# Column tiles of 64 for TensorE in a sliding-window attention with a dense block behind it

## The chip, the cores and the metric

The kernel runs on one core of a Trainium2 chip. The core has TensorE (matmuls, from SBUF into PSUM), VectorE, ScalarE, GpSimd and SyncE, which work from queues of their own and wait for one another through semaphores. The metric is the device time of one launch in microseconds (us), as the median of several runs. One further look is taken by the hardware profiler: its span runs from the first to the last instruction of one execution.

In the profile TensorE has two rows: PE for the matmul itself, which streams the moving operand through the array, and PEld for the load of the stationary operand ("weights") before it. A form such as "128\*128 128x512" gives the rows and columns of the stationary operand, and then partitions and columns of what is written.

## The reference

```python
# q, k, v: (8 batches, 8 heads, 576 positions, 64)
scores = q @ k.T / sqrt(64)
scores = where(abs(pos_q - pos_k) <= 32, scores, -1e9)
attn = exp(scores - max(scores)); attn /= sum(attn) + 1e-9
x = (attn @ v), heads side by side          # (8 * 576 = 4608 tokens, 512)
h = x @ w_in                                # (4608, 2048)
out = (relu(h) ** 2) @ w_out                # (4608, 512), float32
```

All arrays are given and returned in float32; the kernel's operands of TensorE are bfloat16, its sums in PSUM float32.

## The kernel before

**Attention.** Each batch is cut into 9 chunks of 64 queries, 72 steps n in all. The window of a chunk is 128 keys wide. `scores` (L471) computes the scores transposed, keys on partitions: for each of four pairs of heads j one matmul with the keys of the pair as stationary operand (128 keys in its columns) and the queries of both heads as 128 moving columns, where zeros in the unused rows of QZ keep the heads apart. ScalarE takes the exponential of all 512 columns (L484), and VectorE multiplies by the mask of the window into P (L491). P has for each pair of heads three blocks of 64 columns: head a, a block of zeros, head b.

`av` (L494) computes P V. For each pair of heads two matmuls add up in PSUM (L506, L507): columns [a, 0] of P as stationary operand against the values of head a, then [0, b] against those of head b. So rows 0 to 63 of the result are the 64 queries of head a and rows 64 to 127 those of head b. The moving operand has 64 value columns and one of ones, whose result is the sum for the softmax; VectorE takes its reciprocal (L522) and multiplies (L524) into XR. The zero blocks are written once, by `setup_ptz` (L305).

`xturn` (L529) turns XR so that features lie on partitions: for the first 28 steps by two transposes of TensorE into TRP (L542) and a copy by ScalarE, later by a DMA that SyncE issues.

**Q and K.** For the first two batches, `fine_turn` (L333) turns Q and K by TensorE: groups of 16 transposes with 48 stationary rows and 48 moving columns (L344). For the other batches VectorE transposes them in blocks (L434), and DMAs of SyncE spread them (L446, L454).

**Dense block.** A tile T is 512 tokens. For the first two tiles `mm1_small` (L551) works on 128 tokens at a time: 16 matmuls with 128 moving columns (L561). For the others `mm1` (L577) makes four matmuls with 512 moving columns for each of 16 slices of the hidden width (L584). ScalarE applies Relu, VectorE squares. `mm2` (L596) multiplies by w_out: 16 matmuls with 512 moving columns for each 128 tokens (L602), in four groups. ScalarE copies the result, SyncE stores it.

**Order.** Every operation is recorded with its engine, what it reads and writes, a due time (`key`) and an assumed duration (`dur`). `Prog.schedule` (L76) runs a list schedule over these and fixes the order on each engine; `emit` (L189) writes the instructions in that order with the waits that are needed. Attention is due 12 steps ahead of the dense block. In gaps that the plan leaves on TensorE early on, filler matmuls on zeros are placed (`idle`, L277); they write a PSUM buffer that nobody reads before it is overwritten. All durations are the planner's own numbers, 240 for the P V of a step, 230 for its scores, 864 for four matmuls of 512 columns.

A transfer is named by the queue that issues it: POOL for loads from memory, SP for the rest.

Of the kernel before, what the change touches and what calls it, by code (L numbers as in the profile page):

```python
# [7 lines left out]
BF16 = mybir.dt.bfloat16  # L8
# [9 lines left out]
VE = D_ + 1  # L18
# [6 lines left out]
TOFF, TST, TREL = 6, 0.9, 9  # L25
NQ = 48
PC = 4 * NQ


class Op:  # L30
# [198 lines left out]
class Gen:  # L229
# [5 lines left out]
    def alloc(self):  # L235
        nc = self.nc
        sb, ps = nc.alloc_sbuf_tensor, nc.alloc_psum_tensor
        self.SC = [ps(f"sc{i}", [128, 512], F32) for i in range(2)]
        self.AVP = ps("avp", [128, 512], F32)
        self.TRP = ps("trp", [128, 1024], BF16)  # L240
        self.HT = [ps(f"ht{i}", [128, 512], F32) for i in range(2)]
        self.OUTP = [ps(f"outp{i}", [128, 512], F32) for i in range(2)]

        self.RAW = {t: [sb(f"{t}raw{i}", [128, 9, 4, 64], BF16) for i in range(2)] for t in "qk"}
        self.ST = {t: sb(f"{t}st", [128, 2, 1152], BF16) for t in "qk"}
        self.QZ = [sb(f"qz{i}", [128, 4, 2, S_], BF16) for i in range(2)]
        self.KT = [sb(f"kt{i}", [128, 4, KW], BF16) for i in range(2)]
        self.VD = [sb(f"vd{i}", [128, 4, H_, VS], BF16) for i in range(2)]
        self.VX = [sb(f"vx{i}", [128, 5, H_, VS], BF16) for i in range(2)]
        self.MASK = [sb(f"mask{i}", [128, 64], BF16) for i in range(3)]  # L250
        self.ID = sb("ident", [128, 128], BF16)
        self.E = [sb(f"e{i}", [128, 512], BF16) for i in range(2)]
        self.PT = [sb(f"pt{i}", [128, 4 * 192], BF16) for i in range(2)]
        self.RS = [sb(f"rs{i}", [128, 4], F32) for i in range(2)]
        self.XR = [sb(f"xr{i}", [128, 256], BF16) for i in range(4)]
        self.XT = sb("xt", [128, NSTEP, 4, 64], BF16)
        self.W1 = sb("w1", [128, 4, DFF], BF16)
        self.W2 = sb("w2", [128, 16, DM], BF16)
        self.GT = [sb(f"gt{i}", [128, 16, 512], BF16) for i in range(2)]
        self.RT = [sb(f"rt{i}", [128, 512], BF16) for i in range(4)]  # L260
        self.ZZ = sb("zz", [128, 512], BF16)
        self.OE = [sb(f"oe{i}", [128, 512], F32) for i in range(3)]
# [10 lines left out]
    def setup_idle(self):  # L273

        self.ms("DVE", ["zz"], self.ZZ[:], 0.0, -1000, 200)
        self.p.idle_on = self.p.ops[-1]
        self.p.idle = lambda e: e.matmul(self.OUTP[1][:], self.ZZ[:, 0:128], self.ZZ[:], start=True, stop=True)  # L277

    def setup_id(self, key):
        self.ms("DVE", ["id"], self.ID[:], 1.0, key)  # L280
# [13 lines left out]
    def setup_rest(self, i, key):  # L294
# [6 lines left out]
        self.ms("DVE", [("vdone", i)], self.VD[i][:, :, :, 64:VS], 1.0, key, 120)  # L301
        self.ms("DVE", [("ktpad", i, 0)], self.KT[i][:, :, 0:32], 0.0, key)
        self.ms("DVE", [("ktpad", i, 1)], self.KT[i][:, :, 32 + S_:KW], 0.0, key)

    def setup_ptz(self, i, key):  # L305
        for j in range(4):
            self.ms("DVE", [("ptz", i)], self.PT[i][:, 192 * j + 64:192 * j + 128], 0.0, key, 70)

    def setup_qz(self, i, key, rows, old=()):

# [160 lines left out]
    def scores(self, n):  # L471
        b, c = divmod(n, NCH)
        i = b % 2
        sc = self.SC[n % 2]
        key = n - LEAD

        def f(e):
            for j in range(4):
                mm = e.matmul(sc[:, 128 * j:128 * j + 128], self.KT[i][:, j, 64 * c:64 * c + 128],  # L479
                              self.QZ[i][:, j, :, 64 * c:64 * c + 64], start=True, stop=True)  # L480
            return mm

        self.p.rec("PE", f, reads=self.qk_tags(b, c), writes=[("sc", n % 2)], key=key, dur=230)
        self.p.rec("ACT", lambda e: e.activation(self.E[n % 2][:], sc[:], ACTF.Exp, scale=0.125),  # L484
                   reads=[("sc", n % 2)], writes=[("e", n % 2)], key=key, dur=560)
        mi = 1 if c == 0 else (2 if c == NCH - 1 else 0)
        msk = self.MASK[mi]
        pt = bass.AP(self.PT[n % 2], 0, [[768, 128], [192, 4], [128, 2], [1, 64]])
        ee = bass.AP(self.E[n % 2], 0, [[512, 128], [128, 4], [64, 2], [1, 64]])
        mb = bass.AP(msk, 0, [[64, 128], [0, 4], [0, 2], [1, 64]])  # L490
        self.p.rec("DVE", lambda e: e.tensor_tensor(pt, ee, mb, ALU.mult),  # L491
                   reads=[("e", n % 2), ("mask", mi)], writes=[("pt", n % 2)], key=key, dur=430)

    def av(self, n):  # L494
        b, c = divmod(n, NCH)
        i = b % 2
        s = c // 2
        key = n - LEAD
        vt = self.VX[i][:, s] if c % 2 == 0 else self.VD[i][:, s]
        pt = self.PT[n % 2]  # L500

        def f(e):
            for j in range(4):
                ha = 4 * (j // 2) + j % 2
                o = self.AVP[:, VE * j:VE * j + VE]
                e.matmul(o, pt[:, 192 * j:192 * j + 128], vt[:, ha, 0:VE], start=True, stop=False)  # L506
                mm = e.matmul(o, pt[:, 192 * j + 64:192 * j + 192], vt[:, ha + 2, 0:VE], start=False, stop=True)  # L507
            return mm

        if c % 2 == 0:  # L510
            rd = [("vdone", i)]
            if s in (0, 4):
                rd += [("vx", i, s)]
            if s > 0:
                rd += [("vxl", i, s)]
            if s < 4 and not (b < 2 and s == 0):
                rd += [("vxh", i, s)]
        else:
            rd = [("vd", i, s), ("vdone", i)]
        self.p.rec("PE", f, reads=rd + [("pt", n % 2), ("ptz", n % 2)], writes=["avp"], key=key, dur=240)  # L520
        rs, xr = self.RS[n % 2], self.XR[n % 4]
        self.p.rec("DVE", lambda e: e.reciprocal(rs[:], bass.AP(self.AVP, 64, [[512, 128], [VE, 4]])),  # L522
                   reads=["avp"], writes=[("rs", n % 2)], key=key - 0.1, dur=160)
        self.p.rec("DVE", lambda e: e.tensor_tensor(  # L524
            bass.AP(xr, 0, [[256, 128], [64, 4], [1, 64]]), bass.AP(self.AVP, 0, [[512, 128], [VE, 4], [1, 64]]),
            bass.AP(rs, 0, [[4, 128], [1, 4], [0, 64]]), ALU.mult),
            reads=["avp", ("rs", n % 2)], writes=[("xr", n % 4)], key=key - 0.1, dur=430)

    def xturn(self, n):  # L529

        xr = self.XR[n % 4]
        key = n - LEAD
        old = [("fraw", 1, t, x) for t in "qk" for x in (1, 2)] if n >= 40 else []
        if n >= NPE:
            self.p.rec("SP", lambda e: e.dma_start(
                self.XT[:, n].rearrange("p (j h) q -> p j (h q)", j=2), xr[:], transpose=True),
                reads=[("xr", n % 4)], writes=[("xt", n)], dma=(f"x{n % 4}", n), key=key, dur=1000, move=(16, 20), old=old)
            return

        def f(e):  # L540
            for t in range(2):
                mm = e.transpose(self.TRP[:, 128 * t:128 * t + 128], xr[:, 128 * t:128 * t + 128], self.ID[:])  # L542
            return mm

        self.p.rec("PE", f, reads=[("xr", n % 4), "id"], writes=["trp"], key=key, dur=112)
        self.p.rec("ACT", lambda e: e.activation(self.XT[:, n], self.TRP[:, 0:256].rearrange("p (f q) -> p f q", f=4),
                                                 ACTF.Copy),
                   reads=["trp"], writes=[("xt", n)], key=key, dur=370)


    def mm1_small(self, T, g, q, key):  # L551
# [3 lines left out]
        ht, rt, gt = self.HT[k % 2], self.RT[k % 4], self.GT[T % 2]  # L555
        t0 = 512 * T + 128 * g

        def f(e):
            for d in range(4 * q, 4 * q + 4):
                for ft in range(4):  # L560
                    mm = e.matmul(ht[:, 128 * (d % 4):128 * (d % 4) + 128], self.W1[:, ft, 128 * d:128 * d + 128],  # L561
                                  self.XT[:, t0 // 64:t0 // 64 + 2, ft, :], start=(ft == 0), stop=(ft == 3))
            return mm

        self.p.rec("PE", f, reads=[("xt", 8 * T + 2 * g), ("xt", 8 * T + 2 * g + 1), ("w1", q)], writes=[("ht", k % 2)], key=key,
# [11 lines left out]
    def mm1(self, T, d, key):  # L577
# [3 lines left out]

        def f(e):
            for ft in range(4):
                mm = e.matmul(ht[:], self.W1[:, ft, 128 * d:128 * d + 128], self.XT[:, 8 * T:8 * T + 8, ft, :],  # L584
                              start=(ft == 0), stop=(ft == 3))
            return mm

        self.p.rec("PE", f, reads=[("xt", 8 * T + j) for j in range(8)] + [("w1", d // 4)], writes=[("ht", k % 2)],
# [7 lines left out]
    def mm2(self, T, u, seg, key):  # L596
# [2 lines left out]

        def f(e):  # L600
            for d in range(4 * seg, 4 * seg + 4):
                mm = e.matmul(op[:], gt[:, d, 128 * u:128 * u + 128], self.W2[:, d, :], start=(d == 0), stop=(d == 15))  # L602
            return mm

        self.p.rec("PE", f, reads=[("gt", T % 2, d, u) for d in range(4 * seg, 4 * seg + 4)] + [("w2", seg)],
# [10 lines left out]
    def build(self):  # L616
        p = self.p
# [6 lines left out]
        self.fine_load(0, "q", 0, K + 1)  # L624
        self.setup_id(K + 0.5)
        self.setup_rest(0, K + 1)
        self.setup_ptz(0, K + 1)
        self.setup_ptz(1, K + 1)
        self.load_ve(0, K + 2, False)
        self.setup_mask(1, K + 2.5)  # L630
        self.load_w1(0, K + 4)
# [115 lines left out]
```

## Time and profile before

| | before |
|---|---|
| median of three runs | 335.07 us |
| the three runs | 334.23, 335.07, 339.73 us |
| span of the profiled execution | 329.7 us |
| what lies around the span (median less span) | 5.4 us |
| TensorE busy, matmul | 312.8 us, 2707 instructions |
| TensorE busy, weight load | 176.9 us, 2707 instructions |
| VectorE busy | 201.8 us |
| ScalarE busy | 172.8 us |
| GpSimd busy | 82.5 us |
| mean granted clock of TensorE | 0.995 of full |

The profiled execution's whole time is not listed beside its span, so the fourth row is a difference against the median. Busy times overlap, and matmuls overlap one another: their ends are modelled, with a tail behind the stream. The rate of TensorE is therefore read from the starts of its instructions. The chain of work that ended last goes back from the last instruction, at each step to what released it, and says which work set the end. The waits say who waited for whom.

### The profile page before, as it was taken

The page shows a single profiled execution, that of the slowest core. Times are in us where ns is not written, and L with a number is a line of the kernel's source. Part 1 is how long each engine was busy: PE and PEld are TensorE (multiplying, and loading weights), DVE is VectorE, ACT ScalarE, POOL GpSimd, SP SyncE. Part 2 cuts the span into 40 slices and gives each one's busy share as a digit, 9 for nine tenths or more (in the row PEclk, how much of TensorE's full clock was granted, in tenths as well). Part 3 has the DMA queues.
Part 4 walks back from the last instruction along what each step waited for, and adds up shares of the span by engine and source line. Part 5 has one row for each costly group of instructions (what it writes and reads, how often), then busy time and mean ns, then how long its engine had stood idle before and what let it go on. Part 6 is the DMA issues. An engine that isn't in the chain of part 4 may idle for free.

```text
span 329.7 us, 6908 instructions
## 1 busy us (share of the span) xinstructions
PE 312.8 (95%) x2707; PEld 176.9 (54%) x2707; DVE 201.8 (61%) x461; ACT 172.8 (52%) x313; POOL 82.5 (25%) x130
## 2 busy tenths in 40 slices
PE   7699897999799999989899999999999999999996
PEld 3356496786685555445455555555555554444442
DVE  7546564989689788779777767777544442222200
ACT  2366279965574764555264555554455554434411
POOL 8999253125053242405321110000000000000000
PEclk9989999999999999999999999999999999999999
DMA  8999999999999999799999668333311111100012
GB/s 92 173 202 203 193 150 184 182 237 199 213 184 164 210 144 126 94 224 172 173 196 150 125 123 148 89 85 84 86 49 48 51 55 55 43 32 34 32 72 88
DMA packets 89376, 42.53 MB, mean 129 GB/s; under 512 B 54528, under 2 KB 83840, under 8 KB 89344
## 3 DMA queue, kind: packets, MB, share of 16 engines
q0 software_dynamic: 62272, 18.49, 61.1%
q1 hardware_dynamic: 27072, 23.60, 28.2%
q8 instruction: 21, 0.34, 0.5%
q14 instruction: 11, 0.09, 0.1%
HBM read 36.96 MB, written 9.44 MB: 141 GB/s over the span
## 4 chain that ended last, share of the span: by engine, by line
PE 81%; DMA 7%; DVE 6%; ACT 2%; issue 1%; POOL 1%; SPq 1%; ACTq 0%
PE outp L602 34%; PE ht L584 28%; PE ht L561 7%; PE sc L479 5%; DMA qz<-qst 4%; DMA qraw<-in_k_dram 2%; PE avp L507 2%; PE avp L506 2%; DVE qz L266 2%; PE outp L277 1%; DMA xt<-xr 1%; PE sc L344 1%; PE trp L542 1%; DVE qst L434 1%; SPq L454 1%
## 5 line engine op out<-in xcount | busy, mean ns | idle before, releaser
L602 PE MATMUL outp<-w,gt 128*128 128x512 bf16 x576 | 143.1, 379 | 0.9 <-DVE gt L570 0.9
L584 PE MATMUL ht<-xt,w 128*128 128x512 bf16 x448 | 113.5, 379 | 0.9 <-DMA xt<-xr 0.9
L590 ACT ACTIVATE rt<-ht 128x512 bf16<-128x512 f32 x112 | 66.9, 597 | 80.9 <-PE ht L584 77.7
L602 PEld LDWEIGHTS outp<-w,gt 128*128 128x128 bf16 x576 | 53.7, 98 | 59.1 <-DVE gt L570 1.5
L592 DVE TENSOR_TENSOR gt<-rt 128x512 bf16<-128x512 bf16 x112 | 46.3, 420 | 50.0 <-ACT rt L590 49.4
L584 PEld LDWEIGHTS ht<-xt,w 128*128 128x128 bf16 x448 | 40.7, 98 | 40.1 <-DMA xt<-xr 1.4
L484 ACT ACTIVATE e<-sc 128x512 bf16<-128x512 f32 x72 | 41.6, 596 | 18.5 <-PE sc L479 12.4
L381 POOL DMA_DIRECT2D vd<-in_v_dram x32 | 28.8, 911 | 84.0 <-PE avp L507 63.3
L491 DVE TENSOR_TENSOR pt<-e,mask 128x512 bf16<-128x512 bf16 x72 | 29.9, 416 | 16.5 <-ACT e L484 15.9
L434 DVE STREAM_TRANSPOSE kst<-kraw 128x640 bf16<-128x640 bf16 (+1 forms) x24 | 35.0, 1457 | 0.6 <-DMA kt<-kst 0.6
L434 DVE STREAM_TRANSPOSE qst<-qraw 128x640 bf16<-128x640 bf16 (+1 forms) x24 | 35.1, 1462 | 0.0
L611 ACT ACTIVATE oe<-outp 128x512 f32<-128x512 f32 x36 | 21.6, 600 | 24.8 <-PE outp L602 24.8
L561 PE MATMUL ht<-xt,w 128*128 128x128 bf16 x512 | 32.8, 219 | 1.3 <-issue 0.7
L524 DVE TENSOR_TENSOR xr<-avp,rs 128x256 bf16<-128x256 f32 x72 | 30.2, 420 | 1.9 <-DVE rs L522 0.2
L522 DVE RECIPROCAL rs<-avp 128x4 f32<-128x4 f32 x72 | 13.2, 184 | 29.5 <-PE avp L507 28.8
L561 PEld LDWEIGHTS ht<-xt,w 128*128 128x128 bf16 x512 | 29.3, 98 | 3.4 <-ACT rt L567 1.2
L479 PE MATMUL sc<-qz,kt 128*128 128x128 bf16 x288 | 25.9, 219 | 4.9 <-DMA qz<-qst 3.4
L479 PEld LDWEIGHTS sc<-qz,kt 128*128 128x128 bf16 x288 | 19.8, 98 | 15.9 <-DMA qz<-qst 4.4
L567 ACT ACTIVATE rt<-ht 128x512 bf16<-128x512 f32 x32 | 19.0, 600 | 7.3 <-PE ht L561 6.3
L277 PE MATMUL outp<-zz 128*128 128x512 bf16 x59 | 18.0, 437 | 1.3 <-DVE zz L266 1.3
L360 ACT ACTIVATE qz<-sc 64x384 bf16<-64x384 bf16 x24 | 14.3, 596 | 9.3 <-PE sc L344 8.8
L506 PE MATMUL avp<-vx,pt 128*128 128x65 bf16 x160 | 15.1, 192 | 2.6 <-DMA vx<-in_v_dram 2.6
(51 smaller groups left out, 220.6 us busy)
## 6 DMA issues: line engine op xcount, KB each, us to landing
out_dram<-oe SPq DMA_DIRECT2D x36, 256.0 KB, 2.3
vd<-in_v_dram POOLq DMA_DIRECT2D x32, 128.0 KB, 8.2
qraw<-in_q_dram POOLq DMA_DIRECT2D x24, 144.0 KB, 7.4
kraw<-in_k_dram POOLq DMA_DIRECT2D x24, 144.0 KB, 8.3
qz<-qst SPq DMA_DIRECT2D x48, 72.0 KB, 3.5
kt<-kst SPq DMA_DIRECT2D x24, 144.0 KB, 4.6
vx<-vd SPq DMA_DIRECT2D x12, 264.0 KB, 4.9
w<-in_moe_w_in_dram POOLq DMA_DIRECT2D x4, 512.0 KB, 11.1
```

The costliest lines, as they stand in the source:

```text
L381: self.p.rec("POOL", lambda e, s=s: e.dma_start(self.VD[i][:, s, :, 0:64], v[b, :, 32 + 128 * s:160 + 128 * s, :].rearrange("h p d -> p h ...
L434: self.p.rec("DVE", lambda e: e.transpose(dst, src), reads=[("raw", t, i, g) for g in range(4)], writes=[("st", t, dh, m0)], key=key, dur= ...
L479: mm = e.matmul(sc[:, 128 * j:128 * j + 128], self.KT[i][:, j, 64 * c:64 * c + 128], self.QZ[i][:, j, :, 64 * c:64 * c + 64], start=True, ...
L484: self.p.rec("ACT", lambda e: e.activation(self.E[n % 2][:], sc[:], ACTF.Exp, scale=0.125), reads=[("sc", n % 2)], writes=[("e", n % 2)], ...
L491: self.p.rec("DVE", lambda e: e.tensor_tensor(pt, ee, mb, ALU.mult), reads=[("e", n % 2), ("mask", mi)], writes=[("pt", n % 2)], key=key, ...
L506: e.matmul(o, pt[:, 192 * j:192 * j + 128], vt[:, ha, 0:VE], start=True, stop=False)
L524: self.p.rec("DVE", lambda e: e.tensor_tensor(bass.AP(xr, 0, [[256, 128], [64, 4], [1, 64]]), bass.AP(self.AVP, 0, [[512, 128], [VE, 4], [ ...
L561: mm = e.matmul(ht[:, 128 * (d % 4):128 * (d % 4) + 128], self.W1[:, ft, 128 * d:128 * d + 128], self.XT[:, t0 // 64:t0 // 64 + 2, ft, :], ...
L584: mm = e.matmul(ht[:], self.W1[:, ft, 128 * d:128 * d + 128], self.XT[:, 8 * T:8 * T + 8, ft, :], start=(ft == 0), stop=(ft == 3))
L590: self.p.rec("ACT", lambda e: e.activation(rt[:], ht[:], ACTF.Relu), reads=[("ht", k % 2)], writes=[("rt", k % 4)], key=key, dur=560)
L592: self.p.rec("DVE", lambda e: e.tensor_tensor(gt[:, d, :], rt[:], rt[:], ALU.mult), reads=[("rt", k % 4)], writes=[("gt", T % 2, d, u) for ...
L602: mm = e.matmul(op[:], gt[:, d, 128 * u:128 * u + 128], self.W2[:, d, :], start=(d == 0), stop=(d == 15))
```

## The change

A helper `halves` takes the place of a plain matmul: it issues two, the first with stationary columns 0 to 63 into the output's partitions 0 to 63, the second with columns 64 to 127 into partitions 64 to 127. Both stream the whole moving operand. It is used by the scores, by both forms of the first dense product, by the second one, and by the filler matmuls. The two transposes of a step's XR become four in the same way. The Q, K turns of the first two batches are left as they are.

In P V the pair of heads no longer adds up in one 128-row result. Each head has a matmul of its own with 64 stationary columns of P, into its own half of the partitions, and P is stored without the zero blocks, as 512 columns in one piece. The memsets of the zero blocks and the wait on them go. The planner's duration of a step's P V is 130 in place of 240; the other durations stay.

```diff
+def halves(e, out, w, x, start, stop):
+    for r in (0, 64):
+        mm = e.matmul(out[r:r + 64], w[:, r:r + 64], x, start=start, stop=stop)
+    return mm
...
-        self.PT = [sb(f"pt{i}", [128, 4 * 192], BF16) for i in range(2)]
+        self.PT = [sb(f"pt{i}", [128, 512], BF16) for i in range(2)]
...
-        self.p.idle = lambda e: e.matmul(self.OUTP[1][:], self.ZZ[:, 0:128], self.ZZ[:], start=True, stop=True)
+        self.p.idle = lambda e: halves(e, self.OUTP[1][:], self.ZZ[:, 0:128], self.ZZ[:], True, True)
...
-    def setup_ptz(self, i, key):
-        for j in range(4):
-            self.ms("DVE", [("ptz", i)], self.PT[i][:, 192 * j + 64:192 * j + 128], 0.0, key, 70)
...
             for j in range(4):
-                mm = e.matmul(sc[:, 128 * j:128 * j + 128], self.KT[i][:, j, 64 * c:64 * c + 128],
-                              self.QZ[i][:, j, :, 64 * c:64 * c + 64], start=True, stop=True)
+                mm = halves(e, sc[:, 128 * j:128 * j + 128], self.KT[i][:, j, 64 * c:64 * c + 128],
+                            self.QZ[i][:, j, :, 64 * c:64 * c + 64], True, True)
...
-        pt = bass.AP(self.PT[n % 2], 0, [[768, 128], [192, 4], [128, 2], [1, 64]])
-        ee = bass.AP(self.E[n % 2], 0, [[512, 128], [128, 4], [64, 2], [1, 64]])
-        mb = bass.AP(msk, 0, [[64, 128], [0, 4], [0, 2], [1, 64]])
+        pt = self.PT[n % 2][:].rearrange("p (h q) -> p h q", h=8)
+        ee = self.E[n % 2][:].rearrange("p (h q) -> p h q", h=8)
+        mb = bass.AP(msk, 0, [[64, 128], [0, 8], [1, 64]])
...
                 ha = 4 * (j // 2) + j % 2
-                o = self.AVP[:, VE * j:VE * j + VE]
-                e.matmul(o, pt[:, 192 * j:192 * j + 128], vt[:, ha, 0:VE], start=True, stop=False)
-                mm = e.matmul(o, pt[:, 192 * j + 64:192 * j + 192], vt[:, ha + 2, 0:VE], start=False, stop=True)
+                for u in range(2):
+                    mm = e.matmul(self.AVP[64 * u:64 * u + 64, VE * j:VE * j + VE],
+                                  pt[:, 128 * j + 64 * u:128 * j + 64 * u + 64], vt[:, ha + 2 * u, 0:VE],
+                                  start=True, stop=True)
...
-        self.p.rec("PE", f, reads=rd + [("pt", n % 2), ("ptz", n % 2)], writes=["avp"], key=key, dur=240)
+        self.p.rec("PE", f, reads=rd + [("pt", n % 2)], writes=["avp"], key=key, dur=130)
...
             for t in range(2):
-                mm = e.transpose(self.TRP[:, 128 * t:128 * t + 128], xr[:, 128 * t:128 * t + 128], self.ID[:])
+                for r in (0, 64):
+                    mm = e.transpose(self.TRP[r:r + 64, 128 * t:128 * t + 128],
+                                     xr[:, 128 * t + r:128 * t + r + 64], self.ID[:])
...
-                    mm = e.matmul(ht[:, 128 * (d % 4):128 * (d % 4) + 128], self.W1[:, ft, 128 * d:128 * d + 128],
-                                  self.XT[:, t0 // 64:t0 // 64 + 2, ft, :], start=(ft == 0), stop=(ft == 3))
+                    mm = halves(e, ht[:, 128 * (d % 4):128 * (d % 4) + 128], self.W1[:, ft, 128 * d:128 * d + 128],
+                                self.XT[:, t0 // 64:t0 // 64 + 2, ft, :], ft == 0, ft == 3)
...
-                mm = e.matmul(ht[:], self.W1[:, ft, 128 * d:128 * d + 128], self.XT[:, 8 * T:8 * T + 8, ft, :],
-                              start=(ft == 0), stop=(ft == 3))
+                mm = halves(e, ht[:], self.W1[:, ft, 128 * d:128 * d + 128], self.XT[:, 8 * T:8 * T + 8, ft, :],
+                            ft == 0, ft == 3)
...
-                mm = e.matmul(op[:], gt[:, d, 128 * u:128 * u + 128], self.W2[:, d, :], start=(d == 0), stop=(d == 15))
+                mm = halves(e, op[:], gt[:, d, 128 * u:128 * u + 128], self.W2[:, d, :], d == 0, d == 15)
...
-        self.setup_ptz(0, K + 1)
-        self.setup_ptz(1, K + 1)
```

## The prediction

> **What bounds the kernel now.** I read the page's busy times first, then the chain of work that ended last, then TensorE's waits, and last the timeline of TensorE at three places, because the busy time of an engine whose matmuls overlap says little about its rate.
>
> ```profile
> span 329.7 us, 6908 instructions
> PE 312.8 (95%) x2707; PEld 176.9 (54%) x2707; DVE 201.8 (61%) x461; ACT 172.8 (52%) x313; POOL 82.5 (25%) x130
> ...
> PE 81%; DMA 7%; DVE 6%; ACT 2%; issue 1%; POOL 1%; SPq 1%; ACTq 0%
> PE outp L602 34%; PE ht L584 28%; PE ht L561 7%; PE sc L479 5%; DMA qz<-qst 4%; DMA qraw<-in_k_dram 2%; PE avp L507 2%; PE avp L506 2%; DVE qz L266 2%; PE outp L277 1%; DMA xt<-xr 1%; PE sc L344 1%; PE trp L542 1%; DVE qst L434 1%; SPq L454 1%
> ```
>
> TensorE is busy for 95% of the span and carries 81% of the chain; the two dense products (L602, L584) alone are 62% of it. P V, the only part whose arithmetic shrinks, is the two entries avp L506 and L507, 4% together. The windows show where TensorE still stands idle (first column the stretch, second its length, third TensorE's busy time):
>
> ```profile
> 0.00:20.00 20.00, 15.19 (x131) 7.52 (x132) 13.34 (x47) 7.50 (x12) 18.41 (x37) 0.91 1.20 145
> 20.00:40.00 20.00, 18.05 (x210) 11.05 (x207) 10.58 (x26) 10.21 (x20) 15.25 (x22) 1.00 1.43 203
> 40.00:60.00 20.00, 17.83 (x319) 15.58 (x320) 11.21 (x28) 16.59 (x34) 7.70 (x12) 1.00 2.22 171
> 60.00:80.00 20.00, 19.41 (x267) 14.30 (x266) 18.08 (x33) 14.83 (x31) 5.43 (x8) 1.00 1.68 201
> 80.00:100.00 20.00, 18.00 (x268) 14.81 (x264) 16.49 (x34) 12.52 (x24) 7.32 (x12) 1.00 1.32 206
> ...
> 200.00:240.00 40.00, 40.00 (x287) 20.75 (x286) 27.50 (x59) 20.94 (x36) 0.24 (x1) 1.00 0.38 95
> ```
>
> Idle time is 4.8 + 2.0 + 2.2 + 0.6 + 2.0 = 11.6 us in the first 100 us and none from 200 us on. So a nanosecond per matmul, gained or lost, reaches the end almost whole after 100 us, and in part before. The rates come from the starts in TensorE's timeline (start us, us with the modelled tail, count at the end):
>
> ```profile
> 41.33 1.95 PE L561 MATMUL ht<-xt,w 128*128 128x128 bf16 x32
> 43.11 0.28 PE L542 MATMUL trp<-ident,xr 128*128 128x128 bf16 x2
> ...
> 43.47 1.95 PE L561 MATMUL ht<-xt,w 128*128 128x128 bf16 x32
> 45.35 0.57 PE L344 MATMUL sc<-ident,kraw 48*128 48x48 bf16 x16
> 45.76 0.55 PE L344 MATMUL sc<-ident,qraw 48*128 48x48 bf16 x16
> 46.25 0.34 PE L542 MATMUL trp<-ident,xr 128*128 128x128 bf16 x2
> ...
> 201.75 1.03 PE L602 MATMUL outp<-w,gt 128*128 128x512 bf16 x4
> 202.61 1.03 PE L584 MATMUL ht<-xt,w 128*128 128x512 bf16 x4
> 203.47 0.19 PE L506 MATMUL avp<-vx,pt 128*128 128x65 bf16 x1
> 203.50 0.20 PE L507 MATMUL avp<-vx,pt 128*128 128x65 bf16 x1
> ...
> 203.69 0.19 PE L507 MATMUL avp<-vx,pt 128*128 128x65 bf16 x1
> 203.71 0.59 PE L602 MATMUL outp<-w,gt 128*128 128x512 bf16 x2
> ```
>
> Each spacing is the time to the next group's start divided by the count, and includes the load of that matmul's own weights. At 512 columns it is (203.47 - 202.61)/4 = 215 ns. At 128 columns, (43.11 - 41.33)/32 = 55.6 ns. P V with 65 columns, (203.71 - 203.47)/8 = 30 ns. The Q, K turns with 48 columns, (45.76 - 45.35)/16 = 25.6 ns, the closest together that two pairs of load and matmul stand in this trace. From 512 to 128 columns the time falls with the streamed columns (215 to 55.6, ratio 3.9). A dense matmul is thus bound by its stream, with the load hidden; at 48 columns something else, load or issue, sets 25.6.
>
> **The change part by part.** The counts, by the groups:
>
> ```profile
> L602 PE MATMUL outp<-w,gt 128*128 128x512 bf16 x576 | 143.1, 379 | 0.9 <-DVE gt L570 0.9
> L584 PE MATMUL ht<-xt,w 128*128 128x512 bf16 x448 | 113.5, 379 | 0.9 <-DMA xt<-xr 0.9
> L602 PEld LDWEIGHTS outp<-w,gt 128*128 128x128 bf16 x576 | 53.7, 98 | 59.1 <-DVE gt L570 1.5
> L561 PE MATMUL ht<-xt,w 128*128 128x128 bf16 x512 | 32.8, 219 | 1.3 <-issue 0.7 <-ACT xt L546 0.2
> L479 PE MATMUL sc<-qz,kt 128*128 128x128 bf16 x288 | 25.9, 219 | 4.9 <-DMA qz<-qst 3.4 <-ACT qz L360 1.5
> L542 PE MATMUL trp<-ident,xr 128*128 128x128 bf16 x56 | 7.9, 222 | 1.2 <-DVE xr L524 1.1
> ```
>
> *512 columns.* 576 + 448 = 1024 matmuls become 2048 halves with 64 stationary columns; each half still streams all 512 columns. If two halves run beside each other in the two column tiles, a pair lasts as long as one stream, 215 ns, and nothing changes; one after the other it is 430. The trace has no column-tiled matmul, so these are the two ends: 0 and 1024 x 215 = +220 us. I take 0: in the rows above TensorE already overlaps the load of one matmul (98 ns in its record) with the stream of the one before, so neighbouring instructions on different parts of the array are its ordinary work. In a stream of in-order halves the second starts one spacing after the first, 25.6 ns by the turns, and both then repeat every 215; two spacings are 51 ns, far below 215.
>
> A page of the Trainium skill supports this: "TensorE: Matmul & The Clock Gate", section "Measured speedup vs the span model", gives 2.38 times for three column tiles at 512 columns, and some 4 ns between the tiles' starts; no run here shows it, and with it the 512-column term would be 0 as well.
>
> *128 columns.* 512 + 288 + 56 = 856 matmuls (first dense product of the first tiles, scores, turns of x) become 1712 halves. A pair lasts the longer of its stream, 55.6 ns, and two spacings, 51.2 ns by the turns: no change, but with 4 ns of room only. If a half takes s, the cost is 1712 x (s - 27.8) ns from s = 27.8 on.
>
> *P V.* Eight matmuls of 128 stationary columns become eight of 64, so the count stays, and each pair may run in two tiles. Before: 0.24 us a group, 72 groups, 17.3 us. After, in spacings of the turns: 8 x 25.6 = 0.205 us, a gain of 72 x 0.035 = 2.5 us. Lower end: each pair costs one spacing of a P V matmul, 4 x 30 = 0.12 us, a gain of 72 x 0.12 = 8.6 us. Upper end: a half with its own load is as slow as one whole 128-column matmul, 55.6 ns: 8 x 55.6 = 0.445 us, 72 x 0.205 = +14.8 us. I take the turns' 25.6, since it is the only row in which something other than the stream sets the spacing.
>
> *Turns among tiled matmuls.* The Q, K turns stay whole, so the array changes its shape around them. A change shows today: 45.35 - 43.47 - 32 x 0.0556 = 0.10 us ahead of a turn, 46.25 - 45.76 - 16 x 0.0256 = 0.08 behind it. The code makes 12 groups of 16 turns, so that is at most 24 x 0.1 = 2.4 us, which stays; at worst it doubles. I take 0.
>
> *The load of weights* is where a rule speaks against the change. By "TensorEngine Tiling (Array Packing)", section "Restrictions", column tiling turns off the fast weight load; by "TensorE: Matmul & The Clock Gate", section "LDWEIGHTS (loading the stationary operand)", a load then takes its columns divided by 1.2 ns, an estimate of 53 ns for 64 columns. By that price, in series, the sum would be 1712 x 25.5 + 576 x 23.3 = +57 us. The trace cannot decide it: it shows 128-column loads that fit into 25.6 ns and none of 64. The mechanism is the second rival below.
>
> *VectorE, P.* The product with the mask keeps its 512 elements and only loses the holes in its output; the square of the dense product, which has none, takes as long. The eight memsets of P's zero blocks go.
>
> ```profile
> L491 DVE TENSOR_TENSOR pt<-e,mask 128x512 bf16<-128x512 bf16 x72 | 29.9, 416 | 16.5 <-ACT e L484 15.9
> L592 DVE TENSOR_TENSOR gt<-rt 128x512 bf16<-128x512 bf16 x112 | 46.3, 420 | 50.0 <-ACT rt L590 49.4
> L266 DVE MEMSET pt<- 128x32 uint32 x8 | 0.4, 85 | 0.0
> ```
>
> At 416 against 420 ns the mask's product gains nothing. The memsets, 0.4 us on an engine busy 13.3 of the first 20 us, lie beside the loads that the first P V waits for (below): 0, at most -0.4 us.
>
> *Order.* The planner is told 130 instead of 240 ns for a P V, 72 x 0.11 = 7.9 us of TensorE in all, so groups behind may be placed earlier or otherwise. What can come of it lies in the idle time of the first 100 us. The waits of TensorE (us in total, times, longest) say what ends it:
>
> ```profile
> PE sc L479 <- DMA qz<-qst: 3.4, 2, 2.0
> PE avp L506 <- DMA vx<-in_v_dram: 2.6, 1, 2.6
> PE sc L479 <- ACT qz L360: 1.5, 2, 1.3
> ```
>
> These three, 7.5 us, end on transfers and on ScalarE, not on P V; I put the reordering at 0, with 3 us either way (half of the transfers' 6.0). No wait is added anywhere; the only one removed is that on the zero blocks. No DMA is added or moved by hand. The filler matmuls of L277 write a buffer nobody reads, between real work: 0 as a pair, and one more stream each where halves run in series.
>
> *Sum.* 0 + 0 - 2.5 + 0 = -2.5 us on a span of 329.7 us. The time around the span is not itemised; the median of the runs, 335.07, is 5.4 us above it, and I leave that alone: 332.5 us. Two per cent, 6.7 us, is about what a measurement of this kernel can tell from no change. The likeliest case's own upper end: each pair may cost some issue time, which I bound by the difference of the two small spacings, 30 - 25.6 = 4.4 ns; on 1880 pairs that is +8.3 us, 340.8.
>
> **The rivals.**
>
> *P V in full pairs.* If the halves of P V run truly beside each other, with loads too, the gain is the 8.6 us above: 326.5 us. For it: the spacing of 25.6 belongs to turns in one and the same place of the array. Against: the loads would have to start in pairs, and the trace shows load, matmul, load, matmul at one spacing each.
>
> *Halves bound by their own loads: slower.* A load of 64 columns in a tile may take longer than the 25.6 ns into which 128 columns fit today. The place is wherever the stream is short: 1712 halves of 128 columns and 576 of P V. With spacing s the cost is 1712 x (s - 27.8) + 576 x (s - 30) ns. The sign turns at 28.4 ns, 2% slower is reached at 31.3 ns. At the nearest row above, 55.6 ns, it is 47.6 + 14.7 = +62 us, 397 us; some of that would fall into the idle 11.6 us. The 512-column pairs don't feel it, two spacings of 55.6 being 111 against 215. For it: the room is 2 ns in 28. Against: the load's record of 98 ns at all 576 of L602 is nowhere seen in a spacing, so loads overlap well. The Trainium skill's rule in the section "Restrictions", above, would act here by this mechanism.
>
> *Halves in series.* The change doesn't do what it says if the array takes the two halves one after the other: +220 us from the 512 columns, 856 x 55.6 = +47.6 us from the others, 0 from P V: 603 us. Any hold between tiles shorter than a whole stream lies between this and 340. For it: no row here has ever shown two matmuls in different column tiles. Against: nothing that this trace shows.
>
> **How the numbers follow.** Forecast (328.5 to 340.8 us): 0.45. P V in full pairs: 0.15, of which 0.13 lies below 328.4. Bound by loads, 341 to 397: 0.27. In series, wholly or in part, above 397: 0.13. Cases of both signs hold most of the chance; the likeliest one's own range is 328.5 to 340.8. The range for 8 in 10 goes from 326.5 up to 397, where the series case (0.13) is left out and a little of the fastest. Faster by over 2%: 0.13; within: 0.47; slower: 0.27 + 0.13 = 0.40.
>
> **What would show it.** In the changed kernel's timeline, groups that write outp with 512 columns and eight halves should still start 860 ns apart; 1720 would be the series case. Thirty-two halves of 128 columns (one group of ht in the first tiles) should take 890 ns; 1780 means loads. A P V group should take 0.2 us, 0.12 if in pairs, 0.44 if bound by loads. The 512-column rate would stay as it is in both of the first two rivals, so it separates them from the third. I am wrong if the halves' spacing leaves 25 to 28 ns, or if TensorE's idle time of the first 100 us grows through the new order.

## The result, and the profile after

| | before | after |
|---|---|---|
| median of four runs each | 334.65 us | 350.76 us |
| lowest to highest | 333.86 to 339.73 us | 345.86 to 353.73 us |
| span of the profiled execution | 329.7 us | 349.7 us |
| mean granted clock of TensorE | 0.995 | 0.956 |

The changed kernel is slower: ratio 1.043, 95% interval 1.032 to 1.053, or 14 us. The ratio leaves out runs over 1.5% above the fastest of their kernel, the profiled one of after among them, so it is not the quotient of the medians. The profiled execution after took 351.43 us in all, 1.7 us more than its span. The 5.4 us that the prediction put around the span of before was therefore partly a profiled execution faster than the median, and the 20.0 us between the spans overstate the 16.1 us between the medians.

The page of the changed kernel, with the rows that answer to those of before; all halved matmuls stand on line 32, the helper's:

```profile
span 349.7 us, 10773 instructions
PE 318.9 (91%) x4646; PEld 201.9 (58%) x4646; DVE 199.2 (57%) x453; ACT 172.9 (49%) x313; POOL 82.6 (24%) x130
...
PEclk9989978799897899999998999999999999999999
...
q8 instruction: 36, 0.59, 0.8%
...
PE 77%; DMA 9%; DVE 6%; issue 5%; SPq 1%; POOL 1%; ACT 0%
```

Three rows have moved: "issue", time in which the engine waited for nothing that the profile shows, from 1% to 5% of the chain; the granted clock, which now has several slices below 9; and queue 8, which carries instructions, to 36 packets. Its row on the page of before (packets, MB, share of 16 engines):

```profile
q8 instruction: 21, 0.34, 0.5%
```

Queue 8 carries TensorE's instructions: before, 2 x 2707 matmuls and loads came in 21 packets, after, 2 x 4646 in 36, which is some 258 a packet both times. The form 128\*64 shows halves with 64 stationary columns each.

TensorE's timeline shows first one of the standstills and then the rates (start us, us with the modelled tail, count at the end, idle time before and what ended it):

```profile
42.90 1.98 PE L32 MATMUL ht<-xt,w 128*64 128x128 bf16 x64
44.81 0.57 PE L346 MATMUL sc<-ident,kraw 48*128 48x48 bf16 x16
45.31 0.25 PE L546 MATMUL trp<-ident,xr 128*64 128x128 bf16 x2
50.05 0.32 PE L546 MATMUL trp<-ident,xr 128*64 128x128 bf16 x2 [4.49 <-issue]
...
202.66 1.03 PE L32 MATMUL outp<-w,gt 128*64 128x512 bf16 x8
203.52 0.29 PE L508 MATMUL avp<-vx,pt 128*64 128x65 bf16 x8
203.65 0.39 PE L32 MATMUL sc<-qz,kt 128*64 128x128 bf16 x8
203.87 1.03 PE L32 MATMUL ht<-xt,w 128*64 128x512 bf16 x8
```

The rates are those of whole matmuls or better. Eight halves of 512 columns take 0.86 us, so a pair takes the 215 ns of one whole matmul. Eight halves of 128 columns take 0.22 us, 55 ns a pair. Eight halves of P V take 0.13 us in place of 0.24. The two tiles run fully beside each other, loads included.

The time is lost elsewhere. TensorE stops in the middle of the four transposes of one step: two start at 45.31 us and end 0.25 us later, and the other two follow 4.49 us after that. Nothing within such a group waits for data. The waits of TensorE (us in total, times, longest) list all standstills of this kind, marked "issue":

```profile
PE ht L32 <- issue: 5.3, 2, 4.8
PE trp L546 <- issue: 4.5, 1, 4.5
PE sc L32 <- DMA qz<-qst: 4.1, 3, 1.8
PE outp L32 <- issue: 3.2, 1, 3.2
PE trp L546 <- DVE xr L527: 2.9, 4, 1.5
```

Standstills without a wait are 5.3 + 4.5 + 3.2 = 13.0 us, in three long pieces at 45, 61 and 106 us and a short one. Before there was one, of 0.7 us. What came while TensorE stood is in the transfers of the changed kernel, in two neighbouring windows, 39.1 to 46.4 us and 46.4 to 48.5 us (packets, MB, share of the 16 engines):

```profile
q0 software_dynamic: 4111, 1.04, 246.1%
...
q0 software_dynamic: 807, 0.25, 257.2%
q8 instruction: 1, 0.02, 6.0%
```

Queue 8 brought nothing for over 7 us, then one packet of 0.02 MB in a window that starts 0.8 us after TensorE stopped and ends 1.5 us before it went on. All that time queue 0, the loads that GpSimd issues, filled the engines: its packets took 246% and 257% of the time of all 16, so more than two were under way at each.

Where the standstills come settles what they wait for. The stretches up to two of them, at 45 and 61 us, count the matmuls and loads that TensorE had started by then (third and fourth column):

```profile
0.00:48.00 48.00, 40.17 (x728) 25.67 (x728) 29.37 (x79) 21.36 (x39) 36.93 (x63) 0.96 1.53 167
0.00:63.00 63.00, 51.26 (x981) 35.23 (x981) 32.83 (x87) 30.74 (x56) 40.48 (x69) 0.92 1.66 168
```

Three of the runs below, with the planner's old duration, with fewer short matmuls and with short halves to the end, also stop after 728 and 981 matmuls, in part in the midst of other groups. These three, the run with extra loads, the kernel of before and the changed one have 19 standstills put down to "issue" between them. Counted in the traces, with TensorE's few semaphore and drain records taken in, each of the 19 comes when TensorE has started a multiple of 256 instructions and 193 more, and it has as many 256s in it as queue 8 had brought packets by then. So TensorE had used up every instruction it had been given, and waited for the next packet.

The windows show what follows (length, TensorE's busy time with its matmuls; the first of the three numbers at the end is the granted clock):

```profile
45.00:50.00 5.00, 0.56 (x18) 0.38 (x13) 2.74 (x6) 0.51 (x1) 1.81 (x3) 0.77 2.64 136
50.00:54.50 4.50, 4.45 (x84) 4.22 (x86) 0.42 (x1) 2.57 (x5) 1.26 (x3) 0.50 2.06 168
54.50:61.00 6.50, 6.49 (x175) 5.34 (x171) 2.73 (x7) 4.88 (x10) 2.25 (x4) 1.00 1.69 188
...
110.00:116.00 6.00, 5.94 (x69) 5.07 (x70) 1.90 (x6) 3.04 (x6) 0.89 (x1) 0.50 0.29 84
...
40.00:120.00 80.00, 64.53 (x1464) 55.16 (x1460) 45.76 (x90) 43.44 (x84) 19.60 (x30) 0.85 1.35 151
```

Behind the standstill at 45 us TensorE works at half clock for 4.5 us, behind that at 106 us for 6. The Trainium skill, "TensorE: Matmul & The Clock Gate", section "HAM oscillation — how this bites in real kernels", says that an idle gap above some 3.4 us puts the array back to half rate. The trace agrees that a standstill does so, but a shorter one was enough: the one at 106 us lasted 3.2 us, and in the 5 us from 45 us a mean clock of 0.77 means that it fell some 2.3 us before their end, when TensorE had stood for 2.1 us. Over the 80 us from 40 to 120 the clock is 0.85. The same stretch of before:

```profile
40.00:120.00 80.00, 75.25 (x1014) 55.83 (x1015) 62.63 (x131) 55.68 (x111) 26.86 (x41) 1.00 1.57 187
```

A clock of 0.85 costs 80 x 0.15 = 12 us of the full rate, some 2 of them while TensorE stood still anyway (the first window: 5 us at 0.77, idle for 4.4). From span to span: standstills 13.0 - 0.7 = +12.3, clock about +10, P V 72 x (0.13 - 0.24) = -7.9. That is +14 of 20; other waits make up part of the rest. Not all of the slow clock follows such standstills: one more stretch at half clock, from 92 to 95.5 us, comes behind two waits for data of 1.5 and 1.0 us.

### The profile page after: what moved, and what is told of

Its sections match the earlier page's. It is cut to its first block, busy times and chain, and to the rows that moved or that the text cites. A ratio compares the mean times of both kernels' runs of the same rounds, so it can differ in the third digit from the quotient of the medians.

```text
span 349.7 us, 10773 instructions
## 1 busy us (share of the span) xinstructions
PE 318.9 (91%) x4646; PEld 201.9 (58%) x4646; DVE 199.2 (57%) x453; ACT 172.9 (49%) x313; POOL 82.6 (24%) x130
## 4 chain that ended last, share of the span: by engine, by line
PE 77%; DMA 9%; DVE 6%; issue 5%; SPq 1%; POOL 1%; ACT 0%
PE ht L32 34%; PE outp L32 33%; PE sc L32 5%; DMA qz<-qst 5%; DMA qraw<-in_k_dram 2%; PE avp L508 2%; DVE qz L272 2%; DMA xt<-xr 2%; DVE qst L436 2%; PE sc L346 1%; PE trp L546 1%; SPq L456 1%; DVE xr L527 1%; DVE kt L365 1%; DVE pt L493 1%
## 5 line engine op out<-in xcount | busy, mean ns | idle before, releaser
L32 PE MATMUL ht<-xt,w 128*64 128x128 bf16 (+1 forms) x1920 | 152.7, 304 | 8.2 <-issue 5.3
L32 PE MATMUL outp<-w,gt 128*64 128x512 bf16 x1152 | 149.2, 387 | 4.3 <-issue 3.2
L32 PEld LDWEIGHTS ht<-xt,w 128*64 128x64 bf16 x1920 | 83.2, 116 | 44.5 <-issue 8.3
L595 ACT ACTIVATE rt<-ht 128x512 bf16<-128x512 f32 x112 | 66.9, 597 | 81.0 <-PE ht L32 80.3
L32 PEld LDWEIGHTS outp<-w,gt 128*64 128x64 bf16 x1152 | 68.9, 112 | 52.8 <-issue 5.2
L597 DVE TENSOR_TENSOR gt<-rt 128x512 bf16<-128x512 bf16 x112 | 46.2, 419 | 53.9 <-ACT rt L595 53.3
L32 PE MATMUL sc<-qz,kt 128*64 128x128 bf16 x576 | 27.7, 225 | 4.1 <-DMA qz<-qst 4.1
L32 PEld LDWEIGHTS sc<-qz,kt 128*64 128x64 bf16 x576 | 23.0, 114 | 12.9 <-DMA qz<-qst 5.7
L551 ACT ACTIVATE xt<-trp 128x256 bf16<-128x256 bf16 x28 | 10.7, 382 | 23.2 <-PE trp L546 23.0
L32 PE MATMUL outp<-zz 128*64 128x512 bf16 x118 | 20.3, 475 | 1.3 <-DVE zz L272 1.3
L575 DVE TENSOR_TENSOR gt<-rt 128x512 bf16<-128x512 bf16 x32 | 12.9, 418 | 10.9 <-ACT rt L572 10.7
L362 ACT ACTIVATE qz<-sc 64x384 bf16<-64x384 bf16 x24 | 14.3, 597 | 9.0 <-PE sc L346 8.5
L546 PE MATMUL trp<-ident,xr 128*64 128x128 bf16 x112 | 10.0, 239 | 7.5 <-issue 4.5
```

The source lines that it names most:

```text
L32: mm = e.matmul(out[r:r + 64], w[:, r:r + 64], x, start=start, stop=stop)
L362: self.p.rec("ACT", lambda e, d=dst, c=src: e.activation(d, c, ACTF.Copy), reads=[tag] + ([w] if par else []), writes=[w], key=key, dur=590)
L546: mm = e.transpose(self.TRP[r:r + 64, 128 * t:128 * t + 128], xr[:, 128 * t + r:128 * t + r + 64], self.ID[:])
L595: self.p.rec("ACT", lambda e: e.activation(rt[:], ht[:], ACTF.Relu), reads=[("ht", k % 2)], writes=[("rt", k % 4)], key=key, dur=560)
L597: self.p.rec("DVE", lambda e: e.tensor_tensor(gt[:, d, :], rt[:], rt[:], ALU.mult), reads=[("rt", k % 4)], writes=[("gt", T % 2, d, u) for ...
```

## The experiments

Theory F: the doubled count of TensorE's instructions is fetched too late while matmuls are short and the transfer queues are full; TensorE stands still, and its clock is halved afterwards. Theory O: the planner's new duration of P V gives another order, and that makes data late.

**The planner's old duration.**

```diff
-        self.p.rec("PE", f, reads=rd + [("pt", n % 2)], writes=["avp"], key=key, dur=130)
+        self.p.rec("PE", f, reads=rd + [("pt", n % 2)], writes=["avp"], key=key, dur=240)
```

> The changed kernel with the planner told 240 ns for a P V again, so that the order of the work is near that of before. Theory F (the doubled count of TensorE instructions is fetched too late where matmuls are short, TensorE stands still for 3 to 5 us at a time, and its clock is halved afterwards): still slower than before by 3 to 5%, 345 to 352 us, with idle time of TensorE that no wait explains and windows at half clock. Theory O (the new order of the planner makes data late): back to 327 to 331 us, clock 0.99.

Measured: 340.6 us, ratio 1.017 (1.010 to 1.025), clock 0.969. Neither range was met. By the two ratios, 1.043 and 1.017, the planner's number is worth 8.5 us of the loss of 14 and the rest of the change 5.8. Standstills are still there, 7.5 us in place of 13.0, behind the same counts of matmuls (TensorE's waits of this run, and its windows):

```profile
PE sc L346 <- issue: 4.0, 1, 4.0
PE trp L546 <- issue: 3.5, 1, 3.5
...
0.00:49.50 49.50, 39.79 (x728) 25.85 (x729) 29.34 (x79) 21.41 (x39) 36.42 (x62) 0.93 1.59 171
0.00:64.50 64.50, 50.87 (x981) 35.43 (x982) 32.52 (x86) 31.40 (x57) 40.58 (x69) 0.89 1.66 172
...
40.00:120.00 80.00, 67.83 (x1605) 54.36 (x1603) 54.17 (x110) 47.94 (x93) 24.42 (x37) 0.94 1.36 162
```

The clock over the same 80 us is 0.94 against 0.85, worth 7 us between the two profiled executions.

**The order alone.** The other half of the same question, on the kernel of before:

```diff
-        self.p.rec("PE", f, reads=rd + [("pt", n % 2), ("ptz", n % 2)], writes=["avp"], key=key, dur=240)
+        self.p.rec("PE", f, reads=rd + [("pt", n % 2), ("ptz", n % 2)], writes=["avp"], key=key, dur=130)
```

> The kernel of before with one number changed: the planner is told 130 ns for a P V, so the order of the work becomes that of the changed kernel while every matmul stays whole. The changed kernel fell from 351 to 341 us when that number went back. If the order is bad by itself: 341 to 345 us here. If the order only hurts together with the doubled instructions (other standstills, other windows at half clock): 332 to 337 us, clock 0.99.

Measured: 338.6 us over ten runs, ratio 1.011 (1.007 to 1.016); between the two ranges. The new order costs 4 us with every matmul whole. TensorE's waits of this run say where:

```profile
PE sc L479 <- DMA qz<-qst: 5.4, 3, 2.2
...
PE trp L542 <- DVE xr L524: 2.4, 3, 1.3
```

The scores wait 2.0 us longer for Q and the turns of x 1.3 us longer than before (3.4 and 1.1). Why this order is worse is not shown. That the plan takes P V for shorter than it is cannot be all of it: in the changed kernel 130 is the true duration (0.13 us), and it costs more there. Order alone +3.8 and the rest of the change in the old order +5.8 make 9.6, and together they cost 14.3 (all by the ratios). The missing 5 us are about as large as the uncertainty of the three ratios together. The third long standstill, at 106 us, and the half clock behind it are there in the changed kernel and not in the run with 240; why was not settled.

**P V alone in tiles.**

```diff
 def halves(e, out, w, x, start, stop):
-    for r in (0, 64):
-        mm = e.matmul(out[r:r + 64], w[:, r:r + 64], x, start=start, stop=stop)
-    return mm
+    return e.matmul(out, w, x, start=start, stop=stop)
...
-                for r in (0, 64):
-                    mm = e.transpose(self.TRP[r:r + 64, 128 * t:128 * t + 128],
-                                     xr[:, 128 * t + r:128 * t + r + 64], self.ID[:])
+                mm = e.transpose(self.TRP[:, 128 * t:128 * t + 128], xr[:, 128 * t:128 * t + 128], self.ID[:])
```

> Only P V runs in column tiles; scores, turns of x and both dense products are whole matmuls again, so TensorE has as many instructions as before. Theory F: no long idle time without a wait, clock 0.99. The P V groups gain 8 us as in the changed kernel, less the change between tile shapes, 72 groups x 0.18 us (0.10 ahead and 0.08 behind, as at the turns) = 13 us at most: 327 to 340 us. Theory O: the order is that of the changed kernel, so it stays at 345 us or more.

Measured: 341.4 us, ratio 1.018 (1.011 to 1.026), clock 0.990. No standstill without a wait is left among TensorE's waits, as theory F had it, with the order of the changed kernel. But the time is 1.4 us above the range. The timeline of this run shows why:

```profile
203.33 1.03 PE L31 MATMUL ht<-xt,w 128*128 128x512 bf16 x4
204.29 0.32 PE L506 MATMUL avp<-vd,pt 128*64 128x65 bf16 x8
204.53 1.04 PE L31 MATMUL outp<-w,gt 128*128 128x512 bf16 x4
```

Four whole matmuls take 0.86 us, so the array was free for P V at 204.19. It starts at 204.29, needs 0.13, and the next matmul starts at 204.53. So 0.10 us is lost ahead and 0.11 behind: a P V group costs 0.34 us against 0.24 whole, 72 x 0.10 = +7 us. By the Trainium skill, "TensorEngine Tiling (Array Packing)", section "Key Properties", a change of the tiling mode drains TensorE; the lost time fits that, and here it is about 0.1 us each way.

**P V alone in tiles, in the order of before.** The same kernel with `dur=240`.

> Only P V in column tiles, and the planner at 240 for it, so in the order of before. The trace of the same edit with 130 showed 0.09 us of idle array ahead of each tiled P V group and 0.10 us behind it, 0.34 us a group in all against 0.24 before: 72 x 0.10 = +7 us. If these changes of shape are the whole price: 338 to 342 us, as with 130 (341.4). If the order had a share of its own there as it has with whole matmuls (+3.8 us): 335 to 338 us.

Measured: 339.2 us, ratio 1.017 (1.009 to 1.025), in the first range. The changes of shape are the larger part; the 2 us between the two runs lie inside their intervals.

**More instructions without tiles.** The kernel of before with two one-column loads ahead of each whole matmul of the scores and of the first tiles' dense product:

```diff
+def whole(e, out, w, x, start, stop):
+    e.ldweights(w[:, 0:1])
+    e.ldweights(w[:, 0:1])
+    return e.matmul(out, w, x, start=start, stop=stop)
```

> The kernel of before, without column tiles and in its own order, with two extra weight loads of one column ahead of each of the 800 whole matmuls of 128 columns (scores, and first dense product of the first two tiles): four instructions a matmul, as many as in the changed kernel there. What is computed is the same. Theory F: idle time of TensorE of several us without a wait between 40 and 110 us and a lower clock, 342 to 355 us. If instead the extra loads just take time in the array, the spacing of 128-column matmuls grows above 56 ns and no standstill appears. Theory O: 335 us, nothing changes.

Measured: 343.8 us, ratio 1.026 (1.018 to 1.034), clock 0.985. TensorE's timeline and waits of this run:

```profile
41.62 2.19 PE L33 MATMUL ht<-xt,w 128*128 128x128 bf16 x32
43.65 0.28 PE L548 MATMUL trp<-ident,xr 128*128 128x128 bf16 x2
...
44.02 1.56 PE L33 MATMUL ht<-xt,w 128*128 128x128 bf16 x22
48.26 0.77 PE L33 MATMUL ht<-xt,w 128*128 128x128 bf16 x10 [2.68 <-issue]
...
PE ht L33 <- issue: 5.9, 3, 2.7
```

Again TensorE stops within a group, after 22 of 32 matmuls, at nearly the same time as in the changed kernel, and with no column tile in the program. The loads also cost time of their own, (43.65 - 41.62)/32 = 63 ns a matmul against 55.6, at most 800 x 8 = 6 us. So both alternatives of the expectation hold side by side. The clock is lower in two short stretches, 0.50 from 49.9 to 53.2 us and from 63.6 to 66.9, behind standstills of 2.7 and 2.6 us. Standstills need many instructions, not tiles.

**Fewer short matmuls.**

```diff
-NSMALL = 2
+NSMALL = 1
```

> The changed kernel with only the first tile of tokens in pieces of 128 tokens; the second tile takes matmuls of 512 columns, which drops 768 of its 1024 halves. Theory F: less to fetch in the stretch from 40 to 110 us; the standstills there shrink from 13 us to under 6, and the time falls to 332 to 342 us, unless the later start of the second tile costs more. Theory O: no change, 345 to 353 us.

Measured: 352.8 us, ratio 1.053 (1.044 to 1.063). The expectation miscounted: the second tile has 512 halves, and 384 of them go (4646 matmuls became 4262). The standstills halve, but the time does not follow. TensorE's waits of this run:

```profile
PE trp L546 <- DVE xr L527: 12.5, 5, 4.3
...
PE ht L32 <- issue: 3.5, 1, 3.5
PE trp L546 <- issue: 3.1, 1, 3.1
```

Standstills are 6.6 us in place of 13.0. But the second tile's matmuls now need all eight steps of attention at once, TensorE has nothing else to do, and waits 12.5 us for x. The run tells nothing about the time that the standstills cost.

**Short halves to the end.** The changed kernel with `dur=240` and

```diff
-NSMALL = 2
+NSMALL = 9
```

> The changed kernel with the planner at 240 for P V, and all nine tiles of tokens in pieces of 128 tokens, so that TensorE takes in short halves to the very end, also where the transfers have gone quiet (behind 220 us). If instructions come too late because the queues for transfers are full: standstills without a wait again before 120 us and none behind 220 us. If TensorE simply takes in four instructions per 56 ns faster than they can be fetched: standstills to the end, and a time above 360 us.

Measured: 351.3 us in one run. The window from 200 to 349 us, of this run first and then of the changed kernel, and the transfers of this run from 250 to 255 us:

```profile
200.00:349.00 149.00, 146.44 (x3332) 110.17 (x3326) 66.86 (x156) 67.97 (x116) 3.22 (x4) 1.00 0.32 76
```

```profile
200.00:349.00 149.00, 146.68 (x1676) 80.75 (x1670) 69.56 (x164) 69.30 (x119) 4.68 (x6) 1.00 0.34 78
```

```profile
q1 hardware_dynamic: 582, 0.36, 30.6%
q8 instruction: 1, 0.02, 1.9%
```

Behind 200 us TensorE takes in twice the matmuls of the changed kernel, 3332 in 149 us or 22 a microsecond, more than the 18 of the changed kernel between 40 and 120 us (1464 in 80), at clock 1.00, and not one wait of TensorE is listed there. All its standstills lie before 125 us, where queue 0 is busy (4426 packets of it come from 200 to 349 us, against 3763 from 59 to 64). The kernel of before ran dry once under full queues (below) at one whole matmul in 55.6 ns, 18 a microsecond. So it is the full transfer queues that make the fetch late, and not the rate by itself, up to 22 matmuls a microsecond; the densest stretch of the changed kernel (175 in 6.5 us, 27 a microsecond) was not reached with empty queues. The time of above 360 us did not come about.

**Halves only where matmuls are long.** The kernel of before in its own order, with halves of the scores and tiled P V from step 28 on, halves of the first dense product from the third tile on and of the second from the second tile on (P keeps its zero blocks, the tiled P V leaves them out; `mms` issues two halves where its first argument is true, and one whole matmul otherwise):

```diff
+LATE = 28
...
+                mm = mms(n >= LATE, e, sc[:, 128 * j:128 * j + 128], ...
...
+                if n >= LATE:
+                    for u in range(2):
+                        mm = e.matmul(self.AVP[64 * u:64 * u + 64, VE * j:VE * j + VE],
+                                      pt[:, 192 * j + 128 * u:192 * j + 128 * u + 64], vt[:, ha + 2 * u, 0:VE],
+                                      start=True, stop=True)
+                    continue
...
+                mm = mms(True, e, ht[:], ...        # mm1, third tile on
+                mm = mms(T >= 1, e, op[:], ...      # mm2
```

> The kernel of before in its own order; halves and tiled P V only from step 28 and from the third tile of tokens on, that is from about 107 us, where few short matmuls are left. 44 of the 72 P V groups gain 0.115 us each, 5 us in all. Theory F: no standstill, clock 0.99, 328 to 331 us, faster than both kernels. If the halves themselves cost something behind 110 us: 334 us or more.

Measured: 331.7 us over twelve runs, ratio 0.992 (0.989 to 0.996): faster than both kernels, but 0.7 us above the range: half of the 5 us came. The window of this run:

```profile
40.00:120.00 80.00, 76.22 (x1102) 56.69 (x1108) 60.99 (x126) 55.33 (x108) 25.84 (x39) 0.98 1.47 180
```

TensorE's timeline of this run:

```profile
210.57 0.29 PE L518 MATMUL avp<-vd,pt 128*64 128x65 bf16 x8
210.69 1.03 PE L37 MATMUL outp<-w,gt 128*64 128x512 bf16 x8
```

The clock is 0.98 over the 80 us, a tiled P V group takes 0.12 us. No long standstill is left; waits put down to "issue" are 0.3 us or less each. One wait grew; from TensorE's waits of this run:

```profile
PE ht L37 <- DMA xt<-xr: 2.6, 1, 2.6
```

The dense product now waits 2.6 us for an x turned by DMA, 0.9 before. Others became shorter, so this does not account for the missing half of the gain, which stays open.

**The same with the planner at 130 from step 28 on.** `dur=130 if n >= LATE else 240`.

> As the kernel with halves from step 28 on, and the planner told 130 for the P V from step 28 on. If the order that comes of the true duration is no worse there: the same 328 to 331 us. If it is worse, as in the changed kernel: 333 us or more.

Measured: 333.0 us, ratio 0.995 (0.991 to 0.999): at the edge of the second range, still faster than before, and not clearly other than with 240. Telling the planner the true duration bought nothing.

## Why the prediction was wrong

The forecast was 332.5 us, and 350.8 came. That it lies in the range of 326.5 to 397 us is luck: it also lies within the bounds in time of the rival "halves bound by their own loads", for which the upper part of the range was made, but that rival's mechanism did not occur.

*512 and 128 columns*, each 0: right. Pairs take 215 and 55 ns. The section "Measured speedup vs the span model" of the Trainium skill's page "TensorE: Matmul & The Clock Gate", which was for it, agrees with the trace in that a pair lasts as long as one.

*P V*, -2.5 us: the gain came, but was limited by the wrong row. The spacing of the turns, 25.6 ns a half, was taken as the closest; the trace has 0.13/8 = 16 ns, and the term is -7.9 us. The rival "P V in full pairs" had this rate (0.12 us a group) and the time wrong.

*Load of weights*: the price by the Trainium skill ("TensorE: Matmul & The Clock Gate", section "LDWEIGHTS (loading the stationary operand)"), an estimate of 53 ns a load in series, does not show; a P V pair with its two loads takes 32 ns in all. Whether the fast load is off cannot be seen here.

*Turns among tiled matmuls*, 0: about right. In the changed kernel a turn has 44.81 - 42.90 - 64 x 0.0278 = 0.13 us ahead of it and 45.31 - 44.81 - 16 x 0.0256 = 0.09 behind, against 0.10 and 0.08 before. That a change of shape costs about 0.1 us each way, as the turns' rows suggested, was confirmed with P V alone, where it comes to 7 us.

*Order*, "0, with 3 us either way": too small. Alone it costs 3.8 us (interval 2.3 to 5.3 from the ratio, which still reaches into the 3), but with the halves 8.5. The prediction looked at which waits end the idle time, on transfers and ScalarE, and took half of the transfers' part as its bound; these waits can also grow, as those of the scores for Q did, from 3.4 to 5.4 us with the order alone.

**The step that failed** is the sum, where "0 + 0 - 2.5 + 0" has no term for the instructions themselves. The prediction counted halves and priced each by its place in the array; that each also has to be fetched, through the same 16 engines that the loads fill, appears nowhere in it. In its place the runs showed 13.0 us of standstills against 0.7 and a clock of 0.85 against 1.00 from 40 to 120 us; in the old order the change still lost 5.8 us although P V gained 7.9, so that the terms which the sum left out came to some 14 us by this estimate. The trace gave a hint. The row of L561 that the prediction quotes has "1.3 <-issue 0.7", and it was not followed up. The timeline of before, and its transfers from 50 to 54 us:

```profile
52.54 1.28 PE L561 MATMUL ht<-xt,w 128*128 128x128 bf16 x20
54.50 0.83 PE L561 MATMUL ht<-xt,w 128*128 128x128 bf16 x12 [0.68 <-issue]
```

```profile
q0 software_dynamic: 1449, 0.55, 172.5%
q8 instruction: 1, 0.02, 2.5%
```

The groups have 16 matmuls, and TensorE stopped after 20: inside the second group. Even at half the instructions it once ran dry in the dense stretch, beside a fetch under full queues. The standstills cost 12 us, and the clock some 10 more, most of it behind them. In "What would show it" only growth of the idle time "through the new order" was named; the growth came for the most part from another source.

## What to carry to other kernels

Count instructions as a cost of their own: where matmuls are short and the transfer queues are full, an idle time of TensorE put down to "issue" inside a group means that the next change must not add instructions there. Column tiles of 64 ran fully in pairs here, but each change between whole and tiled matmuls cost about 0.1 us each way, so they pay where many neighbours can be tiled together and the instruction rate is low. Change a planner's duration in a run of its own; here it was worth at least as much as the edit it came with.

## What was not expected of the hardware

Halves with loads of their own follow one another every 16 ns (eight in 0.13 us), while the closest whole matmuls of the trace before, the turns, stood 25.6 ns apart. A fetch that arrives late costs twice: 4.5 us of standstill, and then 4.5 us at half clock, in which 2.2 us of work are lost. TensorE's instructions come 256 to a packet, and all 19 standstills lie at a border between two packets' worth. And the fetch itself has room: 22 matmuls with their loads in a microsecond ran without a wait once queue 0 was empty.
